# A LayerNorm, linear-attention and MLP block on one core: a new order for every engine, the block map on GpSimd, another queue for one tile, a fourth u tile

## The chip, the cores and the metric

The kernel runs on one core of a Trainium2 chip. The core has five engines with their own instruction queues: TensorE (PE; PEld is its weight load), VectorE (DVE), ScalarE (ACT), GpSimd (POOL) and SyncE (SP, which only issues transfers here). Each runs its queue strictly in order and waits at an instruction until its inputs are there. Transfers are issued from SP's and from ScalarE's queue. The metric is the time of one execution on the device in microseconds; the median of three runs of the kernel before is 239.16 (239.09 to 239.38).

## What is computed

Sequence 2048, width 640, 32 heads of 20, hidden width 1728, all inputs in bfloat16:

```python
qkv = (x @ wqkv) ...                      # q, k, v of 32 heads, 20 wide
pq = einsum("bhsd,hdf->bhsf", q, w_phi)   # pk the same of k
phi_q = concat([softmax(pq), softmax(-pq)])   # phi_k the same of pk
kv = einsum("bhsf,bhsd->bhfd", phi_k, v)
num = einsum("bhqf,bhfd->bhqd", phi_q, kv)
den = einsum("bhqf,bhf->bhq", phi_q, phi_k summed over s) + 1e-6
h  = x + (num / den) @ wo                 # of layernorm(x)
out = h + silu(layernorm(h) @ w1) @ w2
```

## The kernel before

The 2048 rows are 16 tiles of 128 rows (tile number t). All weights stay in SBUF. Nothing is scheduled by a planner at build time: `ORDER` (lines 25 to 64) is a string of words, each word calls one function `op_<name>`, and every engine receives its instructions in the order in which the words stand. `vp.1@6` is `op_vp(1)` with PSUM bank 6 (two-bank results take 6 and 7); there are eight banks. A word's last letter picks the engine or queue: `.a` ScalarE, `.v` DVE, `.p` GpSimd, `.s` SP's queue.

Four stages follow each other and overlap a little.

*Head.* Loads: `lx.a.b` tiles a to b-1 of x, `lk` chunks of the K weights (five of 128 rows), `lv` the V weights, `lp` the small weights w_phi. On GpSimd `mk` makes mask5 and `mo` writes the ones columns of ten V tiles. On DVE `ph` (L195) spreads w_phi into `phb`, the block map: 128 x 5 x 8 x 20 elements, the product of w_phi and mask5. TensorE runs dummy matmuls (`wm`, L262), then transposes the K weights (`wt`, five 128x128, L316), `wc` copies them from PSUM, `fk` (L331) multiplies them with phb and `fc` copies the result to Wfk, the K weights with w_phi folded in. For each x tile `st` takes statistics (two L267 and one L268, DVE), `rs` makes 1/std (L275, a pow on GpSimd), `xn` normalizes (L291 on DVE or L296 on ScalarE). The first four tiles are transposed on TensorE (`xt`, L302, copied by `xc`), the other twelve by a transposing DMA on SP's queue (`xd`).

*Projections.* `kp` and `vp` (both L364) multiply a tile with Wfk and with wv; `ke` takes exp of plus and minus pk (ScalarE), `kr` sums and inverts (DVE), `kn` (L407) normalizes: `.p` all 1280 elements on GpSimd, `.q` 960 there and 320 on DVE (L411), `.b` half each. `vc` copies v. `cc` (L420) adds the tile's phi_k, v product into bank 7. `gk` and `gc` make Wfq as `fk` and `fc` made Wfk, from Q weights that `lq` loads transposed; `qp` (L451, `.0` and `.1` two banks, `.2` one) gives pq of four tiles and `qe` (L461) its exp, EqT. `kc` and `km` spread kv into KVBD; `mc` and `mt` make the mask for that on GpSimd and DVE. `close` frees the memory of the stage.

*Attention.* `dp` (L486) multiplies EqT with KVBD into four banks. `dw` (DVE; L500, L501, L507, L510) makes from it `u`, an f32 tile of 128 x 672, and then the four banks are free; u lies in a pool of three buffers. `dr` inverts the denominators (L515), two `do` (L521, DVE or GpSimd) give `o`, and only then is a u buffer free. `td` transposes o by DMA, `op` (L548) multiplies with wo, `oa` (L557, DVE) adds x, `sq` (ScalarE) and `sr` (GpSimd, L570 to L580) make the second LayerNorm's numbers, `hn` normalizes on DVE (L587) or on ScalarE (L595, with one more GpSimd instruction, L592), `hd` transposes by DMA.

*MLP.* `up` (L627, L637) over groups of 2, 4, 4, 4 and 2 tiles, `ua` silu (L649), `yp` (L673) and `yh` (L686) the down projection, `yo` and `yz` the last add and the store.

A pool's buffers and the eight transfer lanes make further waits: a transfer takes one of eight completion lanes in turn, and waits for the transfer before it in the same lane.

Of the kernel before, what the change touches and what calls it, by code (L numbers as in the profile page):

```python
# [64 lines left out]
"""

@with_exitstack
def kernel(
# [40 lines left out]
    first = early.enter_context(tc.tile_pool(name="first", bufs=1, side="right"))  # L109
# [51 lines left out]
    tl = {}  # L161
# [10 lines left out]
    def wk2():  # L172
        return late["work"]
# [17 lines left out]
            base=DH, pattern=[[6 * DH - 128, C], [DH, 8]], channel_multiplier=-1,  # L191
        )

    def op_ph():
        nc.vector.tensor_tensor(  # L195
            phb[:],
            phr[:].unsqueeze(2).to_broadcast([P, C, 8, DH]),
            mask5[:].unsqueeze(3).to_broadcast([P, C, 8, DH]),
            op=ALU.mult,
        )  # L200
# [277 lines left out]
    def op_dp(t):  # L478
        g, i = t // GT, t % GT
        b = at.pop(0)  # L480
        ps = mm[:, b : b + 4, :]
        for s in range(2):
            for r in range(C):
                for k in range(4):
                    lo = 32 * k
                    nc.tensor.matmul(  # L486
                        ps[:, k, (8 * s + H0[r]) * 22 : (8 * s + H0[r] + NJ[r]) * 22],
                        EqT[g][lo : lo + 32, s, r, i * P : (i + 1) * P],
                        KVBD[lo : lo + 32, s, r, 0 : NJ[r], :].rearrange("p j c -> p (j c)"),
                        start=(s == 0 and r == 0),  # L490
                        stop=(s == 1 and r == C - 1),
                        skip_group_check=True,
                    )
        tl["dp", t] = [ps[:, :, 176 * s : 176 * (s + 1)].rearrange("p k (h c) -> p k h c", c=22) for s in range(2)]

    def op_dw(t, how="p"):
        A = tl["dp", t]
        first = A[0][:, :, :, 0:21]
        w = sm.tile([P, 4, 8], F32, name="w")
        nc.vector.reciprocal(w[:], A[1][:, :, :, 21])  # L500
        nc.vector.tensor_tensor(w[:], w[:], A[0][:, :, :, 21], op=ALU.mult)  # L501
        if how == "c":
            kept = wk2().tile([P, 4, 8, 21], F32, name="kept", bufs=1)
            nc.scalar.copy(kept[:], first)
            first = kept[:]
        u = wk2().tile([P, 4, 8, 21], F32, name="u", bufs=3)
        nc.vector.tensor_tensor(  # L507
            u[:], A[1][:, :, :, 0:21], w[:].unsqueeze(3).to_broadcast([P, 4, 8, 21]), op=ALU.mult,
        )
        nc.vector.tensor_tensor(u[:], u[:], first, op=ALU.add)  # L510
# [229 lines left out]
```

## Time and profile before

| what | value |
|---|---|
| median of 3 runs | 239.16 us (239.09 to 239.38) |
| the profiled execution | 238.86 us |
| its span, first to last instruction | 237.2 us |
| TensorE busy | 229.9 us |
| DVE, ScalarE, GpSimd busy | 133.7, 114.9, 92.9 us |
| first projection matmul | 10.65 us |
| first dp | 69.27 us |
| mean of a dw's four DVE instructions | 0.35, 0.19, 0.86, 0.85 us |
| mean of kn with 1280, 960, 640 elements on GpSimd | 2.40, 1.81, 1.86 us |
| do on GpSimd, on DVE | 0.75, 0.49 us |

Times in a row are from the span's start. A line of a timeline gives start, duration, engine, source line, operation, `out<-in`, count, and in brackets the engine's idle time before it and what ended it. In the chain of waits each row is a start, a duration and what ran. In the slices each digit is the busy share of a fortieth of the span in tenths. TensorE's matmuls overlap, and their ends are modelled, so the distance between starts is the better measure of their pace.

### The profile page before, as it was taken

The page shows a single profiled execution, that of the slowest core. Times are in us where ns is not written, and L with a number is a line of the kernel's source. Part 1 is how long each engine was busy: PE and PEld are TensorE (multiplying, and loading weights), DVE is VectorE, ACT ScalarE, POOL GpSimd, SP SyncE. Part 2 cuts the span into 40 slices and gives each one's busy share as a digit, 9 for nine tenths or more (in the row PEclk, how much of TensorE's full clock was granted, in tenths as well). Part 3 has the DMA queues.
Part 4 walks back from the last instruction along what each step waited for, and adds up shares of the span by engine and source line. Part 5 has one row for each costly group of instructions (what it writes and reads, how often), then busy time and mean ns, then how long its engine had stood idle before and what let it go on. Part 6 is the DMA issues. An engine that isn't in the chain of part 4 may idle for free.

```text
span 237.2 us, 6320 instructions
## 1 busy us (share of the span) xinstructions
PE 229.9 (97%) x2672; PEld 147.6 (62%) x2672; DVE 133.7 (56%) x257; ACT 114.9 (48%) x172; POOL 92.9 (39%) x184
## 2 busy tenths in 40 slices
PE   6899999999999999999999999999999999999995
PEld 2677777777544555886754645556654657688762
DVE  3899999899838989988878504321203000220032
ACT  3788998866866575664054254654014240013000
POOL 7656897798923454188071600534000100000000
PEclk9999999999999999999999999999999999999999
DMA  7964768495001849123734411103211100020012
GB/s 209 305 239 92 128 118 184 120 249 175 3 6 31 179 80 197 37 53 62 113 83 86 83 30 28 29 12 75 72 41 55 28 28 3 28 83 3 0 60 83
DMA packets 44845, 20.68 MB, mean 87 GB/s; under 512 B 34448, under 2 KB 44304, under 8 KB 44816
## 3 DMA queue, kind: packets, MB, share of 16 engines
q1 hardware_dynamic: 43728, 19.88, 36.1%
q10 hardware_dynamic: 1088, 0.39, 0.7%
q8 instruction: 21, 0.34, 0.6%
q14 instruction: 8, 0.07, 0.1%
HBM read 9.61 MB, written 2.62 MB: 52 GB/s over the span
## 4 chain that ended last, share of the span: by engine, by line
PE 88%; DVE 4%; POOL 4%; ACT 1%; DMA 1%; issue 1%; DVEq 0%; POOLq 0%
PE mm L673 24%; PE mm L627 23%; PE mm L364 18%; PE mm L548 8%; PE mm L451 7%; PE mm L486 3%; PE mm L420 2%; ACT EqT L461 1%; DMA X<-in_A_x_dram 1%; PE mm L686 1%; DVE u L507 1%; DVE u L510 1%; PE mm L637 1%; POOL RS L275 1%; PE mm L331 1%
## 5 line engine op out<-in xcount | busy, mean ns | idle before, releaser
L627 PE MATMUL mm<-HnT,w 128*128 128x512 bf16 (+1 forms) x325 | 59.1, 337 | 0.0
L649 ACT ACTIVATE shT<-mm 128x1024 bf16<-128x1024 f32 (+2 forms) x29 | 27.7, 963 | 64.3 <-PE mm L627 48.8
L673 PE MATMUL mm<-w,shT 128*128 128x320 bf16 (+2 forms) x416 | 58.5, 299 | 0.0
L673 PEld LDWEIGHTS <-shT 128*128 128x128 bf16 x416 | 39.7, 98 | 17.7 <-issue 0.8
L627 PEld LDWEIGHTS <-w 128*128 128x128 bf16 x325 | 31.3, 98 | 22.8 <-issue 0.3
L694 DVE TENSOR_TENSOR ob<-mm,X 128x640 bf16<-128x640 f32 x15 | 12.0, 817 | 47.0 <-PE mm L673 29.3
L364 PEld LDWEIGHTS <-XnT 128*128 128x128 bf16 x320 | 30.7, 98 | 11.8 <-issue 0.2
L407 POOL TENSOR_TENSOR Ek<-Ek,Sk 128x1280 bf16<-128x1280 bf16 (+2 forms) x16 | 34.6, 2184 | 3.1 <-DVE Sk L400 2.2
L557 DVE SCALAR_TENSOR_TENSOR X<-mm,X 128x640 bf16<-128x640 f32 x16 | 13.1, 823 | 21.5 <-PE mm L548 21.3
L397 DVE TENSOR_REDUCE Sk<-Ek 128x64 f32<-128x1280 bf16 x16 | 23.3, 1456 | 1.6 <-ACT Ek L389 1.6
L548 PE MATMUL mm<-wo,ot 128*128 128x320 bf16 x160 | 23.9, 299 | 0.2 <-ACT EqT L461 0.2
L521 POOL TENSOR_TENSOR o<-u,rd 128x320 bf16<-128x320 f32 x20 | 14.7, 752 | 22.7 <-DVE rd L515 14.4
L364 PE MATMUL mm<-Wfk,XnT 128*128 128x320 bf16 x160 | 23.4, 299 | 0.0
L451 PE MATMUL mm<-XnT,Wfq 128*128 128x512 bf16 x100 | 23.3, 380 | 0.0
L461 ACT ACTIVATE EqT<-mm 128x1024 bf16<-128x1024 f32 (+1 forms) x24 | 19.6, 884 | 7.4 <-PE mm L451 7.4
L364 PE MATMUL mm<-wv,XnT 128*128 128x320 bf16 x160 | 23.2, 299 | 0.0
L389 ACT ACTIVATE Ek<-mm 128x640 bf16<-128x640 f32 x32 | 20.6, 710 | 3.2 <-PE mm L364 2.7
L548 PEld LDWEIGHTS <-ot 128*128 128x128 bf16 x160 | 15.4, 98 | 7.4 <-issue 0.7
L565 ACT ACTIVATE sq<-X 128x640 bf16<-128x640 bf16 x16 | 11.7, 730 | 9.3 <-DVE X L557 7.7
L267 DVE BATCH_NORM_STATS2 stats<-X 128x6 f32<-128x320 bf16 x32 | 13.7, 468 | 3.8 <-DMA X<-in_A_x_dram 3.8
L577 POOL TENSOR_SCALAR hm<-hst,hm 128x1 f32<-128x1 f32 x16 | 4.6, 290 | 28.0 <-ACT sq L565 27.0
L451 PEld LDWEIGHTS <-Wfq 128*128 128x128 bf16 x100 | 9.1, 98 | 9.9
(78 smaller groups left out, 214.0 us busy)
## 6 DMA issues: line engine op xcount, KB each, us to landing
out_dram<-ob SPq DMA_DIRECT2D x15, 160.0 KB, 1.8
w<-in_B_w_dram SPq DMA_DIRECT2D x6, 360.0 KB, 5.2
X<-in_A_x_dram SPq DMA_DIRECT2D x3, 640.0 KB, 6.6
w<-in_B_w_dram SPq DMA_DIRECT2D x5, 320.0 KB, 4.9
wk<-in_A_wqkv_dram SPq DMA_DIRECT2D x4, 160.0 KB, 4.2
wv<-in_A_wqkv_dram SPq DMA_DIRECT2D x1, 480.0 KB, 7.3
wo<-in_A_wo_dram SPq DMA_DIRECT2D x1, 480.0 KB
w<-in_B_w_dram SPq DMA_DIRECT2D x1, 480.0 KB, 4.0
```

Of the source, the lines that this page charges most:

```text
L267: nc.vector.bn_stats(stats[:, k, :], X[:, t, k * 320 : (k + 1) * 320])
L364: nc.tensor.matmul(ps[:, half, 0:320], tok(XnT[t // GT], t)[:, c, :], W[:, c, half * 320 : (half + 1) * 320], start=(c == 0), stop=(c == C ...
L389: nc.scalar.activation(Ek[:, s, :].rearrange("p (a n) -> p a n", a=2), tl["kp", t][:, :, 0:320], AF.Exp, scale=1.0 - 2.0 * s,)
L397: nc.vector.tensor_reduce(Sk[:], tl["ek", t][:].rearrange("p s (h f) -> p (s h) f", f=DH), axis=AX.X, op=ALU.add,)
L407: nc.gpsimd.tensor_tensor(Ek3[:, 0:n], Ek3[:, 0:n], Sk[:, 0:n].unsqueeze(2).to_broadcast([P, n, DH]), op=ALU.mult,)
L451: nc.tensor.matmul(ps[:, k, :], Wfq[:, c, r * P : (r + 1) * P], XnT[g][:, c, :], start=(c == 0), stop=(c == C - 1),)
L461: nc.scalar.activation(E[:, s, rs[0] : rs[-1] + 1, :], tl["qp", g, i][:, 0 : len(rs), :], AF.Exp, scale=1.0 - 2.0 * s,)
L521: (nc.vector if eng == "v" else nc.gpsimd).tensor_tensor(tl["o", t][:, a * 320 : (a + 1) * 320].rearrange("p (h f) -> p h f", f=DH), tl["u ...
L548: nc.tensor.matmul(ps[:, half, 0:320], tl["ot", t][:, c, :], wo[:, c, half * 320 : (half + 1) * 320], start=(c == 0), stop=(c == C - 1),)
L627: nc.tensor.matmul(ps[:, i * W : (i + 1) * W], w1[:, c, fc * P : (fc + 1) * P], HnT[g][:, c, 0:W], start=(c == 0), stop=(c == C - 1), skip ...
L649: nc.scalar.activation(sh[:, a:b], tl["up", g, k][:, 0 : b - a], AF.Silu)
L673: nc.tensor.matmul(ps, shT[g][:, fc * W + i * P : fc * W + (i + 1) * P], w2[:, fc, a:b], start=first and fc == 0, stop=last and fc == FC - ...
```

## The change

`ph` takes an engine as argument, and the new order calls `ph.p`: the product for phb is now GpSimd's. Tile 1 of x (`lx.1.2`) is issued from ScalarE's queue, third there, where the last chunk of the K weights (`lk.4.5`) stood; that chunk now goes last on SP's queue, behind tiles 2 and 3 of x (`lx.2.4`). `mc`, the second mask, stands among the kn on GpSimd rather than in the head. The u pool has four buffers. The variant `how="c"` of `dw` copies the whole PSUM result; every `dw` word in both orders ends in `.p`. `mo` stands before `mk`. The whole order is new: among others 13 kn are `.p` (10 before), one is `.q` (4 before); 11 hn run on ScalarE (7 before), 10 xn (9 before); on TensorE xt.0 comes before wt.2, wt.3, wt.4 and all fk (before: after four of the five fk); the head has three dummies of 256 columns more. Loads of x come as tiles 4 to 7, 12 to 15, 8 to 11 (before: 8 to 11, 4 to 7, 12 to 15).

```diff
-lx.0.1.a lk.0.1.s lp.a lx.1.2.s lk.4.5.a lk.1.2.s lk.2.3.s lk.3.4.s mk mo wm.512@7 wm.512@7 wm.512@7
-wm.512@7 wm.512@7 wm.512@7 wm.512@7 wm.512@7 wm.512@7 wm.256@7 wt.0@0 st.0 rs.0.1 wm.256@2 wm.128@2 wt.4@1
-ph ta mc st.1 wc.0.a wt.1@2 lx.2.4.s wc.1.v fk.0@4 wt.2@3 wc.2.v lx.8.12.s wc.4.a fc.0.a fk.4@6 fc.4.a
-rs.1.2 xn.0.v fk.1@0 fc.1.a wt.3@2 wc.3.v fk.2@4 fc.2.a xt.0@3 xn.1.v xc.0.v st.2 rs.2.3 st.9 fk.3@6 fc.3.a
-xn.2.v xt.1@2 st.8 xc.1.a rs.8.10 kp.0@0 ke.0 kp.1@4 lv.0.3.s ke.1 lv.3.5.s xt.2@3 xc.2.a vp.1@6 lq.1.s st.3
+mo mk lx.0.1.a lp.a lx.1.2.a lk.0.1.s lk.1.2.s st.0 rs.0.1 st.1 ta wm.512@7 wm.512@7 wm.512@7 wm.512@7
+wm.512@7 wm.512@7 wm.512@7 wm.512@7 wm.512@7 wm.256@7 wt.0@0 wc.0.a ph.p xn.0.v lx.2.4.s rs.1.2 wt.1@1
+wc.1.a wm.256@3 xt.0@2 xc.0.a lk.2.3.s wm.256@4 wm.256@4 wm.128@4 wt.2@3 st.2 rs.2.3 wc.2.a xn.1.v wm.256@6
+fk.0@4 lk.3.4.s wt.3@6 wc.3.v fk.1@0 lk.4.5.s lx.4.8.s fc.0.a fc.1.a wt.4@7 wc.4.v lv.3.5.s fk.2@2 fc.2.a
+fk.3@4 fk.4@6 xn.2.v fc.3.v st.3 fc.4.a xt.1@0 rs.3.4 xc.1.a xt.2@1 xc.2.a kp.0@2 ke.0 st.5 kp.1@4 kp.2@6
...
-qe.0.0 qp.0.2@6 cc.7 close kc qe.0.2 qp.3.0@2 l2.4.6.s l2.6.8.s km.1 km.0 dp.0@4 dw.0.p dr.0 do.0.0.p l1.2.s
-l1.3.s qe.3.0 do.0.1.p qp.1.0@0 dp.1@2 qe.1.0 dw.1.p dr.1 do.1.1.p qp.1.1@6 dp.3@0 dw.3.p qe.1.1 do.1.0.v
-dr.3 do.3.0.p do.3.1.p qp.2.0@4 qe.2.0 dp.2@0 dw.2.p dr.2 qp.1.2@6 qe.1.2 td.0 do.2.0.p l1.4.s l1.5.s op.0@4
+gk.4@2 cc.6 ke.10 cc.0 cc.12 kn.8.p cc.5 gc.4.a l1.4.s kp.13@4 ke.13 l2.8.10.s kp.14@0 ke.14 kr.14 qp.0.0@2
+vp.9@4 qe.0.0 l1.2.s vp.10@0 vc.10.a qp.0.1@2 vc.9.a vp.14@0 kn.9.b vc.14.a cc.11 qe.0.1 kn.15.p cc.15
+kn.14.p cc.8 kr.10 kn.10.p cc.10 qp.0.2@6 qe.0.2 kr.13 kn.13.b mt cc.14 cc.9 cc.13 kc km.0 km.1 qp.3.0@4
+qe.3.0 lo.0.2.s close dp.0@0 dw.0.p dr.0 do.0.1.p qp.1.1@6 qe.1.1 dp.1@0 dw.1.p dr.1 qp.2.0@4 do.0.0.p
+do.1.1.v qe.2.0 dp.3@0 dw.3.p qp.1.0@6 dr.3 do.3.1.v qp.2.2@4 l2.2.4.s dp.2@0 qe.1.0 dw.2.p dr.2 qp.1.2@5
+lh.s qe.2.2 td.0 do.1.0.p td.1 op.0@6 oa.0 do.3.0.p td.3 qe.1.2 dp.4@0 dw.4.p l2.4.6.s sq.0 do.2.0.p op.1@4
+qp.2.1@6 oa.1 dr.4 do.4.1.v dp.6@0 sr.0 dw.6.p dr.6 hn.0.a do.2.1.p td.2 do.4.0.p qe.2.1 sq.1 sr.1 hn.1.v
+qp.3.1@4 qe.3.1 op.3@6 qp.3.2@0 qe.3.2 td.4 oa.3 sq.3 do.6.1.v do.6.0.p dp.5@2 dw.5.p op.2@6 oa.2 op.4@0
+oa.4 dp.9@2 sr.3 hd.0 dw.9.p hd.1 dr.5 up.0.2@6 ua.0.2 l1.1.s hn.3.a dr.9 up.0.3@0 ua.0.3 l2.6.8.s td.6
+do.5.0.v dp.7@2 dw.7.p up.0.0@6 ua.0.0 op.6@0 dr.7 dp.13@2 do.5.1.p td.5 oa.6 do.9.1.p do.9.0.p dw.13.p
...
-    def op_ph():
-        nc.vector.tensor_tensor(
+    def op_ph(eng="v"):
+        (nc.vector if eng == "v" else nc.gpsimd).tensor_tensor(
...
-        first = A[0][:, :, :, 0:21]
+        if how == "c":
+            kept = wk2().tile([P, 4, 352], F32, name="kept", bufs=1)
+            nc.scalar.copy(kept[:], tl["ps", t])
+            A = [kept[:, :, 176 * s : 176 * (s + 1)].rearrange("p k (h c) -> p k h c", c=22) for s in range(2)]
...
-        u = wk2().tile([P, 4, 8, 21], F32, name="u", bufs=3)
+        u = wk2().tile([P, 4, 8, 21], F32, name="u", bufs=4)
...
-        nc.vector.tensor_tensor(u[:], u[:], first, op=ALU.add)
+        nc.vector.tensor_tensor(u[:], u[:], A[0][:, :, :, 0:21], op=ALU.add)
```

More of the change, by code (lines that the diff above doesn't have):

```diff
@@ new lines @@
+lx.8.12.s xd.5 st.13 vp.2@4 xn.7.a vc.2.a kp.3@0 xd.4 xd.7 vp.1@2 xn.6.v lq.2.s lq.0.s rs.12.14 st.8 st.11
+st.10 rs.10.12 st.9 rs.8.10 kr.1 vp.3@4 kn.1.p ke.3 xd.6 ke.2 vp.5@0 vc.5.a xn.11.a xn.13.v vp.4@6 vc.3.a
+vc.4.a kp.5@0 ke.5 kr.3 kn.3.p vc.1.a xn.8.a kp.7@4 ke.7 kp.4@6 ke.4 gk.0@0 vp.7@2 vc.7.a st.15 xd.11 xn.9.a
+vp.11@4 st.14 rs.14.16 xn.15.a kr.2 kn.2.p kr.4 kn.4.p vc.11.v kr.7 kr.0 kn.7.p gc.0.a l1.0.s vp.6@6 mc
+xn.12.a xn.10.v kp.11@2 ke.11 kn.0.p kp.6@4 l1.3.s vc.6.a kr.5 xn.14.a xd.13 vp.13@0 lq.1.s xd.8 kp.8@2
@@ new lines @@
+l2.10.13.s vc.13.a cc.3 l1.5.s ke.6 kr.6 cc.4 kn.6.p kr.11 cc.1 cc.2 cc.7 kn.5.p ke.8 xd.9 kp.9@0 ke.9 xd.12
+kp.12@4 ke.12 kr.12 kn.12.p gk.2@2 gc.2.a xd.15 kp.15@0 ke.15 vp.15@4 kr.8 vp.12@2 vc.15.a gk.1@0 gc.1.a
+vp.8@4 vc.8.a lo.2.5.s xd.10 kp.10@0 vc.12.a l2.0.2.s lq.3.s gk.3@4 gc.3.a xd.14 kn.11.q lq.4.s kr.9 kr.15
+gk.4@2 cc.6 ke.10 cc.0 cc.12 kn.8.p cc.5 gc.4.a l1.4.s kp.13@4 ke.13 l2.8.10.s kp.14@0 ke.14 kr.14 qp.0.0@2
+vp.9@4 qe.0.0 l1.2.s vp.10@0 vc.10.a qp.0.1@2 vc.9.a vp.14@0 kn.9.b vc.14.a cc.11 qe.0.1 kn.15.p cc.15
@@ new lines @@
+yp.0.1 yo.0 yp.1.0 yo.1 td.7 dp.14@4 dw.14.p up.1.1@0 ua.1.1 do.8.1.p dr.14 up.1.6@2 ua.1.6 do.8.0.p sq.6
+sr.6 do.14.0.v dp.10@4 dw.10.p up.1.0@0 ua.1.0 up.1.5@2 sq.9 hn.6.v hd.6 do.14.1.p ua.1.5 up.1.2@4 do.12.0.v
+ua.1.2 op.7@6 oa.7 dp.11@0 td.8 up.1.4@4 dw.11.p dr.10 do.10.1.v up.1.3@6 ua.1.3 do.12.1.p td.14 do.13.1.v
+dr.11 td.12 op.14@0 oa.14 sq.7 ua.1.4 op.8@2 oa.8 sq.8 op.12@6 yp.3.0@0 yp.5.0@4 sr.8 do.10.0.p td.10 td.13
+oa.12 yh.1.0@2,6 yh.1.1 hn.8.a hd.8 yp.5.1 yo.5 yp.2.1 sr.9 hn.9.v sr.7 hn.7.a hd.9 hd.7 yp.3.1 yo.3 op.10@4
@@ new lines @@
+yp.2.0 yo.2 yp.4.1 oa.10 up.2.6@0 ua.2.6 dp.15@2 dw.15.p yp.4.0 yo.4 op.13@0 dr.15 do.15.0.v do.11.0.p
+up.2.0@2 up.2.4@4 ua.2.4 up.2.1@6 ua.2.1 oa.13 up.2.2@0 do.11.1.v ua.2.2 sq.14 do.15.1.p sr.14 sq.13 sr.13
+td.15 sq.12 sr.12 up.2.5@4 ua.2.5 up.2.3@6 td.11 op.11@0 ua.2.0 ua.2.3 yp.9.0@4 yp.6.0@2 op.15@6 yp.6.1
+oa.11 sq.10 sr.10 hn.13.a hd.13 sq.11 hn.12.a hd.12 hn.14.v hd.14 oa.15 sq.15 sr.11 hn.11.a hd.11 yh.2.0@0
+yo.6 hn.10.v hd.10 sr.15 yh.2.1@6 hn.15.a hd.15 yp.7.1 yp.7.0 yp.8.0 yp.9.1 yo.9 up.3.4@2 yp.8.1 yo.7
@@ L65 @@
+up.4.0@4 ua.4.0 up.4.2@6 up.3.1@4 ua.3.4 ua.3.1 up.3.0@2 up.4.3@4 yo.8 ua.3.0 ua.4.3 up.3.3@0 up.3.2@2
+ua.3.2 ua.4.2 up.4.1@4 ua.4.1 up.3.6@2 ua.3.6 yh.4.0@6,4 yp.14.0 up.3.5@2 yp.15.1 yp.15.0 yp.14.1 yo.14
+ua.3.3 ua.3.5 yp.11.1@0 yp.10.1@2 yp.10.0 yp.12.0@6 yh.3.0 yo.15 yo.10 yh.3.1@4,5 yp.11.0 yo.11 yp.12.1
+yo.12 yp.13.0 yz.13.0.s yp.13.1 yz.13.1.a
 """
@@ L501, in op_dw @@
         nc.vector.tensor_tensor(w[:], w[:], A[0][:, :, :, 21], op=ALU.mult)
[L502 to L505, printed above, removed]
-        u = wk2().tile([P, 4, 8, 21], F32, name="u", bufs=3)
+        u = wk2().tile([P, 4, 8, 21], F32, name="u", bufs=4)
         nc.vector.tensor_tensor(
```

35 lines of the change are left out of this document (4 added, 31 removed).

## The prediction

> **What bounds the kernel now.** I read the page first (shares, slices, chain), then what TensorE waited for, then the timeline of the first 11 us, then the chain through the attention stage.
>
> ```profile
> span 237.2 us, 6320 instructions
> ...
> PE 229.9 (97%) x2672; PEld 147.6 (62%) x2672; DVE 133.7 (56%) x257; ACT 114.9 (48%) x172; POOL 92.9 (39%) x184
> ...
> DVE  3899999899838989988878504321203000220032
> ...
> PEclk9999999999999999999999999999999999999999
> ```
>
> TensorE is busy 97% of the span at full granted clock, and DVE is near 90% until slice 20 (about 120 us). The matmuls that compute something are the same in both kernels, so the time can change only by when dense matmul work begins and by how often TensorE then waits. What it waited for:
>
> ```profile
> PE mm L316 <- DMA wk<-in_A_wqkv_dram: 1.4, 1, 1.4
> PE mm L486 <- DVE u L510: 1.4, 4, 0.5
> PE mm L302 <- DVE xn L291: 0.6, 1, 0.6
> PE mm L548 <- ACT EqT L461: 0.2, 1, 0.2
> ```
>
> Columns: total, times, longest. Two waits lie in the head (1.4 for a weight chunk, 0.6 for xn), five in the attention stage. None lies between 11 and 69 us: the projections run without a gap.
>
> ```profile
> 1.25 0.41 SPq L233 DMA_DIRECT2D X<-in_A_x_dram  x1
> 1.72 0.55 ACTq L233 DMA_DIRECT2D wk<-in_A_wqkv_dram  x1
> 5.02 0.99 DVE L195 TENSOR_TENSOR phb<-phr,mask 128x800 bf16<-128x800 bf16 x1
> 6.24 0.73 PE L316 MATMUL mm<-ident,wk 128*128 128x128 bf16 x10 [1.45 <-DMA wk<-in_A_wqkv_dram]
> 10.25 0.45 PE L302 MATMUL mm<-ident,xn 128*128 128x128 bf16 x5 [0.61 <-DVE xn L291]
> 10.65 2.89 PE L364 MATMUL mm<-Wfk,XnT 128*128 128x320 bf16 x20
> ```
>
> The head ends at 10.65, when kp.0 (L364) starts. Line 4 is wt.4: TensorE stood until 6.24 for the chunk that ScalarE's queue sent third, at 1.72. The first and the last wait of the attention stage, in the chain:
>
> ```profile
> 71.51 0.86 DVE u L510
> 72.38 0.04 issue
> 72.42 0.51 PE mm L486 x34
> ...
> 122.63 0.69 POOL o L521
> 123.33 0.02 issue
> 123.35 0.87 DVE u L507
> 124.22 0.02 issue
> 124.24 0.86 DVE u L510
> 125.11 0.04 issue
> 125.15 0.46 PE mm L486 x35
> ```
>
> dp.1 (72.42) needs the banks that dw.0 frees. dp.10 (125.15) waits for dw.15, whose u tile had to be freed by GpSimd's do.12.1 (L521, 122.63): three u tiles were not enough there.
>
> **The change, part by part.**
>
> *Head.* Tile 1 of x moves from SP's second place to the third place of ScalarE's queue. In the completion events of the trace it landed at 4.3 in the old place; the transfer of the same size in the new place landed at 6.2. Bounds 4.3 and 6.2; I take 6.2, as it is the same queue, place and issue time. In the new order DVE does st.1 before xn.0, so xn.0 now waits for tile 1: 6.2 + 1.15 (two L267, one L268: 3.77 to 4.92) + 0.45 (L291) + 0.05 = xt.0 at 7.9, against 8.72 before. Behind xt.0 TensorE's queue holds, before kp.0: wt.2, wt.3, wt.4, xt.1, xt.2 and xt.0 itself (6 x 0.28, chain), five fk (0.32 each, chain, L331 x6) and four dummies (256 columns about 0.11, one of 128: 0.38 in all). Sum 3.66, so 11.55, and 0.1 because the last fk needs wc.4 (0.49 on DVE) right behind wt.4: kp.0 at 11.65. Before, kp.0 started at 10.65 with xt.2 still to do (0.28). The head costs 11.65 - 0.28 - 10.65 = **+0.7** (with the 4.3 bound: xn.0 is then set by GpSimd's pow, xt.0 near 6.9, kp.0 near 10.7, so -0.2; an upper end of +1.2 if the landing slips by 0.5).
>
> What is hidden there: the block map phb on GpSimd. Nearest rows: L407 (1280 elements, bf16, 4.67 for two, 1.8 ns an element) gives 1.45; L521 (320 elements, 0.75) gives 1.9. I take 1.45, the row with the same output type. It starts behind rs.0.1, between 6.1 (pow from 5.17, 0.55 as its other single-column rows, L277 0.26) and 6.8 (pow 1.24, as it was beside DVE's phb), and ends by 8.7 at the latest; fk.0 wants it at 8.8 (xt.0 7.9 plus 0.9 of transposes and dummies). What covers it is the late xt.0; with an early tile 1 it would cost up to 0.5. The last wk chunk now waits for a DMA lane and is issued at about 3.76. Before, the X transfer issued at 3.76, with the same bytes up to its end, landed at 9.1; wt.4 wants the chunk at 9.75. Moving mo ahead of mk costs nothing: GpSimd does both before 4.5, and the pow comes at 5.17.
>
> [...]
>
> *Projections, 11 to 69 us.* DVE loses phb (0.99) and three L411 parts (0.45 each). GpSimd gains three kn of 1280 instead of 960 elements (2.31 - 1.81 = 0.5 each), phb, and the second mask (2.5 us, 6.71 to 9.20 before) in the middle of its kn chain. In 12.2 to 66.9 GpSimd was busy 44.4 of 54.7 us, so the room is there on average. The end decides: kp.14 ends near 56.1, ke.14 and kr.14 (1.3 + 1.95) let kn.14 start at 59.4; kn.14, kn.10, kn.13 (2.3, 2.3, 1.9, with 0.6 for kr.10) end at 66.5; cc.13 stands at 67.4. Slack 0.9; before, the last kn ended 0.2 ahead of cc.7. DVE had 4.4 us of idle there and gets more. ScalarE (45.3 of 54.7) gains one xn (0.82). SP's twelve xd and five lq keep their number; the first due, xd.5, is issued near 17 and lands in 2.6 for vp.5 near 22.8. Cost 0.
>
> *Attention stage, 69 to 126 us.* The waits view shows 1.6 us; measured by late starts of the matmuls (the array also drains at each wait) it is 2.3: dp.1 0.45, dp.3 0.27, dp.2 0.37, two for EqT 0.24 and 0.33, the last dp 0.64. In the new order, with dw 2.36 and 3.0 us from a dp to its banks' release: dp.1 (one double qp of 2.16 as cover) keeps 0.45, dp.3 0.35 (0.27 before); do.1.1 is queued on DVE before dw.3, so dw.3 ends 0.25 later, which dp.2 has room for. dp.2 has 3.24 of qp ahead: 0. Both EqT waits go, since op.0 and its followers take banks whose qe is done earlier. up.0.2 gets 0.4: it needs oa.2, which stands on DVE behind dw.5 (2.36). dp.7 0.15, small ones 0.2. The 0.64 goes with the fourth u tile. New sum 1.55, change **-0.75**; bounds -1.5 (only dp.1 and dp.3 left) and 0. Four more hn on ScalarE (0.92 each) lie in a stage where it was busy 31 of 57 us; each adds an L592 (0.26) on GpSimd, 26 of 57.
>
> *The rest.* The `kept` path is not reached: every dw word ends in p. After 126 us the old kernel has no wait and the new order keeps 25 groups of row-tiled matmuls, as before, so those switches cost the same; 0. The tail (last add, last DMA) is unchanged.
>
> **Sum.** +0.7 - 0.75 = about 0 on 238.86 (span 237.2 and 1.66 around it). The median of the runs is 0.3 above that execution, so the forecast for the median is 239.2: no change. A measurement of this kernel can tell about 0.2% (0.48 us) from none.
>
> **Rivals.**
> 1. *Tile 1 lands early* (faster). The old place landed at 4.3, and a queue's turn is not fixed. Head -0.2 to 0, attention -0.75: 238.3; down to 237.7 if the attention waits fall to dp.1 and dp.3. Against it: the third transfer of that queue was late at the same issue time. [...]
> 2. *GpSimd's chain ends last before dp.0* (slower). One mechanism: phb, the mask and 13 full kn make GpSimd late at cc.10 and cc.13. It decides once a full kn averages over 2.45 us (0.9 slack over the six of the last stretch); the mean of L407 in this form is 2.40, the longest 2.60. At 2.60 over the 13, with 2.31 assumed, it is 3.8 less 0.9 late, of which DVE's order hides about half: +1.5, so 240.7. For it: DVE works beside it all the time; against: pairs ran at 2.3.
> 3. *The clock falls in the head* (slower). TensorE now idles from about 4.7 to 7.9, 3.2 us; before, 1.45 us did no harm. At the start the dummies were 0.43 apart until 3.34 and 0.22 after, so 2.5 us at half pace cost 1.25: +1.3, 240.5. [...]
> 4. *The u tile does not help*: its wait returns as another DVE wait. Only the head's +0.7 stays: 239.9.
>
> **How the numbers follow.** Forecast (238.7 to 239.7) 0.40, of it 0.03 faster, 0.30 same, 0.07 slower. Rival 1: 0.27, faster. Rival 2: 0.20, rival 3: 0.08, rival 4: 0.05, all slower. Faster 0.30, same 0.30, slower 0.40. The range runs from rival 1's middle to rival 2's price: 238.0 to 240.7. Forecast's own range: 238.7 to 239.7.
>
> **What would show it.** kp.0 starting near 11.65 with xt.0 near 7.9 behind st.1 (head right); xt.0 before 7.2 (rival 1). The phb multiply at 1.4 to 1.9 us on GpSimd, ended before fk.0. No TensorE wait from 12 to 70 us; one on `Ek` from GpSimd at the last cc would be rival 2. Dummies and transposes at 0.1 us pitch after 7.9: rival 3. In the waits view u at dp.1 and dp.3 only, and none on do. It is wrong if a wait outside these places passes 0.5 us.

## The result and the profile after

The changed kernel takes 242.19 us (median of five runs, 241.06 to 242.63), the kernel before 239.16 (five runs beside it, 239.09 to 239.62). The ratio is 1.0115, 95% interval 1.0086 to 1.0143: 3.0 us slower, where 239.2 us and a range of 238.0 to 240.7 had been forecast. One execution of the third experiment below (243.06 us) counts as slow, and its median and ratio leave it out.

The profiled execution took 242.63 us, 3.77 more than that of the kernel before. First the page of the changed kernel: span, busy times, the slices of DVE and the granted clock.

```profile
span 240.5 us, 6303 instructions
...
PE 230.3 (96%) x2655; PEld 150.0 (62%) x2675; DVE 132.6 (55%) x248; ACT 118.9 (49%) x177; POOL 95.7 (40%) x189
...
DVE  2699999995867998977785741353013120000232
...
PEclk9799999999999999999999999999999999999999
```

TensorE has the same work, and DVE less. What is new is the 7 in the second slice of the clock (6 to 12 us): it was 9 in every slice before. The waits of TensorE in the changed kernel (total, times, longest):

```profile
PE mm L303 <- DVE RS L273: 2.1, 1, 2.1
PE mm L332 <- issue: 1.6, 1, 1.6
...
PE mm L487 <- DVE u L511: 0.7, 2, 0.5
PE mm L628 <- DMA HnT<-hn: 0.6, 1, 0.6
PE mm L452 <- issue: 0.6, 4, 0.2
```

The chunk wait of 1.4 us in the head is gone, and one of 2.1 us ahead of xt.0 stands in its place. The second row is a kind that the kernel before did not have: 1.6 us, once, released by nothing that the profile shows. The last row, by contrast, is no wait: ahead of each of its four matmuls stand two weight loads and one matmul record, so a matmul was not recorded, and the row is absent in kernels 12 and 13 below, whose profiles have one matmul for each load. The timeline of TensorE in the changed kernel, head and then the place of that gap:

```profile
5.77 0.27 PE L263 MATMUL mm<-const-bfloat16-1.0 128*128 128x256 bf16 x1
8.10 0.45 PE L303 MATMUL mm<-ident,xn 128*128 128x128 bf16 x5 [2.06 <-DVE RS L273]
...
9.68 0.74 PE L317 MATMUL mm<-ident,wk 128*128 128x128 bf16 x5
...
13.38 0.84 PE L365 MATMUL mm<-Wfk,XnT 128*128 128x320 bf16 x5
...
45.45 0.32 PE L332 MATMUL mm<-phb,wk 128*128 128x140 bf16 x3
47.40 0.32 PE L332 MATMUL mm<-phb,wk 128*128 128x80 bf16 x3 [1.63 <-issue]
```

xt.0 starts at 8.10 and kp.0 at 13.38. The five transposes of a weight chunk that take 0.45 at full clock (the row at 8.10 is of the same shape) take 0.74 at 9.68: they start 0.107 us apart instead of 0.056. The same head in windows of the changed kernel (busy time of PE, PEld, DVE, ACT, POOL, then the granted clock, the DMA share and GB/s):

```profile
8.00:9.20 1.20, 1.10 (x16) 1.05 (x17) 1.13 (x6) 0.61 (x2) 0.81 (x2) 0.93 0.91 318
9.20:13.30 4.10, 4.10 (x50) 4.10 (x49) 2.35 (x6) 3.04 (x6) 0.94 (x2) 0.60 1.04 399
13.40:17.00 3.60, 3.60 (x30) 2.61 (x28) 3.46 (x12) 3.57 (x7) 0.86 (x3) 1.00 0.20 80
```

By the spacing of the transposes the clock is at half from about 9.0 to 12.4 us, in the densest part of the head. Both marks, the clock and the gap, lie in stages where the prediction had costs of +0.7 and 0.

Where the 3.77 us of the profiled pair come from: kp.0 is 2.73 later (13.38 against 10.65); from there to dp.0 the changed kernel takes 1.30 more (dp.0's first matmul at 73.23 against 69.20), which is 1.80 at the gap, by starts of matmuls, less 0.50; from dp.0 to the end it takes 0.70 less (167.26 against 167.96); and the time outside the span is 2.14 instead of 1.70 (spans of 240.49 and 237.16 in the traces), which is 0.44.

### The profile page after: what moved, and what is told of

It is laid out like the page before. It is cut to its first block, busy times and chain, and to the rows that moved or that the text cites. A ratio compares the mean times of both kernels' runs of the same rounds, so it can differ in the third digit from the quotient of the medians.

```text
span 240.5 us, 6303 instructions
## 1 busy us (share of the span) xinstructions
PE 230.3 (96%) x2655; PEld 150.0 (62%) x2675; DVE 132.6 (55%) x248; ACT 118.9 (49%) x177; POOL 95.7 (40%) x189
## 4 chain that ended last, share of the span: by engine, by line
PE 85%; DMA 4%; DVE 4%; issue 2%; ACT 2%; POOL 0%; ACTq 0%; DVEq 0%; POOLq 0%
PE mm L628 24%; PE mm L674 23%; PE mm L365 18%; PE mm L549 6%; PE mm L452 4%; PE mm L487 2%; DMA X<-in_A_x_dram 2%; PE mm L421 2%; DMA HnT<-hn 2%; PE mm L332 2%; ACT EqT L462 1%; PE mm L638 1%; PE mm L687 1%; DVE u L508 1%; DVE u L511 1%
## 5 line engine op out<-in xcount | busy, mean ns | idle before, releaser
L628 PE MATMUL mm<-HnT,w 128*128 128x512 bf16 (+1 forms) x315 | 57.8, 335 | 1.2 <-DMA HnT<-hn 0.6
L408 POOL TENSOR_TENSOR Ek<-Ek,Sk 128x1280 bf16<-128x1280 bf16 (+2 forms) x16 | 35.7, 2260 | 2.6 <-DVE Sk L401 2.3
L522 POOL TENSOR_TENSOR o<-u,rd 128x320 bf16<-128x320 f32 x20 | 16.0, 808 | 37.3 <-DVE rd L516 30.6
L452 PE MATMUL mm<-XnT,Wfq 128*128 128x512 bf16 x91 | 22.3, 379 | 0.9 <-issue 0.6
L596 ACT ACTIVATE hn<-X,hm 128x640 bf16<-128x640 bf16 x11 | 10.1, 916 | 9.6 <-POOL hm L593 9.5
L508 DVE TENSOR_TENSOR u<-mm,w 128x672 f32<-128x672 f32 x16 | 13.7, 858 | 1.4 <-DVE w L506 0.3
```

Source lines behind the costliest of these rows:

```text
L408: nc.gpsimd.tensor_tensor(Ek3[:, 0:n], Ek3[:, 0:n], Sk[:, 0:n].unsqueeze(2).to_broadcast([P, n, DH]), op=ALU.mult,)
L452: nc.tensor.matmul(ps[:, k, :], Wfq[:, c, r * P : (r + 1) * P], XnT[g][:, c, :], start=(c == 0), stop=(c == C - 1),)
L508: nc.vector.tensor_tensor(u[:], A[1][:, :, :, 0:21], w[:].unsqueeze(3).to_broadcast([P, 4, 8, 21]), op=ALU.mult,)
L522: (nc.vector if eng == "v" else nc.gpsimd).tensor_tensor(tl["o", t][:, a * 320 : (a + 1) * 320].rearrange("p (h f) -> p h f", f=DH), tl["u ...
L628: nc.tensor.matmul(ps[:, i * W : (i + 1) * W], w1[:, c, fc * P : (fc + 1) * P], HnT[g][:, c, 0:W], start=(c == 0), stop=(c == C - 1), skip ...
```

## The experiments

Three theories at the start. A: TensorE's idle stretch ahead of xt.0 makes the clock fall. B: loads that the change issues earlier hold up the transfer by which TensorE gets its instructions, so that it runs dry at 45 us. C: the late tile 1 is the cause of the head. The rival of them all is that the new order itself, with its sequence of matmuls and copies, is slower. Each kernel was timed against the kernel before on the same chip. The mean granted clock of a run tells whether the clock fell: 3.41 us at half of it (0.50 from 9.03 to 12.44 us in the changed kernel) are 1.7 of 237 us, a mean of 0.993.

| | kernel | median (us) | ratio to before, interval | runs below 0.998 in clock |
|---|---|---|---|---|
| | changed kernel | 242.19 | 1.0115 (1.0086 to 1.0143) | 4 of 5 |
| 1 | dummies before xt.0 | 240.76 | 1.0083 (1.0051 to 1.0116) | 1 of 6 |
| 2 | four loads later | 240.68 | 1.0059 (1.0034 to 1.0084) | 7 of 9 |
| 3 | tile 1 on SP's queue | 240.77 | 1.0068 (1.0043 to 1.0093) | 7 of 12 |
| 4 | 2 and 3 | 240.28 | 1.0031 (1.0013 to 1.0050) | 7 of 12 |
| 5 | 1 and 2 | 239.51 | 1.0006 (0.9997 to 1.0016) | 0 of 11 |
| 6 | 4, phb on DVE | 238.06 | 0.9946 (0.9934 to 0.9958) | 0 of 5 |
| 7 | 5, three u tiles | 239.89 | 1.0021 (1.0011 to 1.0030) | 0 of 11 |
| 8 | before, two loads earlier | 240.57 | 1.0060 (1.0043 to 1.0077) | 0 of 6 |
| 9 | 6, loads early again | 238.84 | 0.9979 (0.9962 to 0.9995) | 0 of 12 |
| 10 | before, four u tiles | 239.12 | 0.9994 (0.9985 to 1.0002) | 0 of 11 |
| 11 | before, fewer dummies | 239.52 | 1.0015 (0.9999 to 1.0032) | 1 of 12 |
| 12 | changed, phb on DVE | 241.16 | 1.0075 (1.0050 to 1.0100) | 4 of 6 |
| 13 | 1, lo.2.5 later | 239.55 | 1.0013 (1.0004 to 1.0022) | 0 of 12 |
| 14 | 1, the other three loads later | 240.18 | 1.0041 (1.0027 to 1.0056) | 0 of 6 |

**1. Dummies in the idle stretch.**

```diff
-wc.1.a wm.256@3 xt.0@2
+wc.1.a wm.512@3 wm.512@3 wm.512@3 wm.512@3 wm.512@3 wm.512@3 wm.512@3 wm.512@3 xt.0@2
```

> The changed kernel with eight 512-column dummies where one of 256 columns stood between wt.1 and xt.0, so that TensorE has work from 5.8 to about 7.5 us. Clock theory: the granted clock stays at 1.00 behind xt.0, the transposes of wt.3 and wt.4 come 0.056 us apart instead of 0.107, kp.0 starts near 11.7 instead of 13.38, and the time falls by 1.6 to 1.8, to a median near 240.5. Rival, head late by tile 1 and its own order only: kp.0 stays near 13.4 or comes later by what the dummies add, the median stays at 242.2 or above.

240.76 us, 1.43 less than the changed kernel (1.6 to 1.8 were expected), and the clock fell in one run of six instead of four of five. TensorE in this kernel's head, and the clock in four windows around its gap:

```profile
5.79 1.91 PE L263 MATMUL mm<-const-bfloat16-1.0 128*128 128x512 bf16 x8
8.43 0.45 PE L303 MATMUL mm<-ident,xn 128*128 128x128 bf16 x5 [0.73 <-DVE RS L273]
```

```profile
40.00:44.00 4.00, 3.90 (x177) 3.02 (x177) 3.97 (x4) 3.37 (x6) 3.79 (x7) 1.00 1.40 202
44.00:46.00 2.00, 0.02 (x1) 0.02 (x1) 1.93 (x4) 0.42 (x1) 1.97 (x2) 1.00 0.42 110
46.00:48.00 2.00, 2.00 (x14) 1.48 (x14) 0.54 (x1) 1.28 (x3) 2.00 (x2) 0.65 1.17 289
48.00:50.00 2.00, 2.00 (x10) 1.10 (x8) 1.84 (x2) 0.67 (x4) 1.45 (x1) 0.50 0.93 91
```

The dummies end before tile 1 is ready and leave 0.73 us idle ahead of xt.0, and kp.0 starts at 12.21 instead of 13.38. The one run in which the clock did fall is the profiled one (243.34 us), and there it fell behind the gap at 44 to 46 us, which is 2.08 us long in it: one more case of theory A, at another place, seen in this one profile.

**2. The loads later.** lo.2.5 (480 KB of wo) and l1.5 go behind lq.4; l2.10.13 and l2.0.2 behind td.1.

```diff
-l2.10.13.s vc.13.a cc.3 l1.5.s ke.6
+vc.13.a cc.3 ke.6
-vp.8@4 vc.8.a lo.2.5.s xd.10 kp.10@0 vc.12.a l2.0.2.s lq.3.s gk.3@4 gc.3.a xd.14 kn.11.q lq.4.s kr.9
+vp.8@4 vc.8.a xd.10 kp.10@0 vc.12.a lq.3.s gk.3@4 gc.3.a xd.14 kn.11.q lq.4.s lo.2.5.s l1.5.s kr.9
-td.1 op.0@6
+td.1 l2.10.13.s l2.0.2.s op.0@6
```

> The changed kernel with four weight loads moved later on SP's queue: lo.2.5 and l1.5 behind lq.4, l2.10.13 and l2.0.2 behind td.1. Fetch theory (TensorE ran out of instructions at 45.6 us, because the 16 KB packet that brings the next ones was held up by the transfers of 36 to 45 us): that packet starts before 43, the gap of 1.63 us in gk is gone or below 0.3, and the time falls by 1.3 to 1.8, to a median near 240.6. Rival, a data wait that the trace does not name (the Q weights, a bank, phb): the gap stays within 0.3 of 1.63 and the median at 242.2.

240.68 us; the gap is gone from the waits, and the head is as it was (2.44 us idle ahead of xt.0). Seven runs at a mean clock of 0.984 to 0.993 took 240.42 to 242.29 us, the two at 1.000 took 239.12 and 239.52: a fall costs about 1.4 us here.

**3 and 4. Tile 1 on SP's queue**, second there, and lk.4.5 third on ScalarE's, as before the change; kernel 4 has the later loads as well.

```diff
-lx.0.1.a lp.a lx.1.2.a lk.0.1.s lk.1.2.s
+lx.0.1.a lp.a lk.4.5.a lk.0.1.s lx.1.2.s lk.1.2.s
-fk.1@0 lk.4.5.s lx.4.8.s
+fk.1@0 lx.4.8.s
```

> The changed kernel with tile 1 of x back on SP's second place and the last chunk of the K weights back on ScalarE's third, as before the change. Clock theory: tile 1 lands near 4.3, xn.0 is then set by GpSimd's pow (done at 5.9), xt.0 starts near 7.0, TensorE idles under 2 us ahead of it and the clock stays at 1.00; kp.0 near 10.8; the time falls by 2.3 to 2.6, to a median near 239.7, with the gap in gk left. Rival, the drop has nothing to do with the idle stretch: the clock still falls, kp.0 near 12.4, median near 241.3.

> Both of the edits before this one: tile 1 on SP's second place and the four loads later. If head and fetch are the two losses and nothing else is, they add: kp.0 near 10.8, no gap in gk, the time 4.0 us below the changed kernel's, a median near 238.2, that is 1.0 below the kernel before, which is the gain of the attention stage. Rival, the attention stage's gain was lent by the delays ahead of it: median at 239.0 or above.

Both miss: 240.77 and 240.28 us. Tile 1 lands early (4.65 us in kernel 4), but xt.0 starts at 8.06 all the same, behind 2.20 us of idle. xn.0 in the changed kernel, then DVE and GpSimd in kernel 4:

```profile
7.65 0.39 DVE L292 TENSOR_SCALAR xn<-X,MV,RS 128x640 bf16<-128x640 bf16 x1
```

```profile
6.31 1.70 DVE L291 TENSOR_SCALAR xn<-X,MV,RS 128x640 bf16<-128x640 bf16 x1
```

```profile
6.30 1.52 POOL L195 TENSOR_TENSOR phb<-phr,mask 128x800 bf16<-128x800 bf16 x1
```

xn.0, which takes 0.39 us in the changed kernel, takes 1.70 here: it starts with phb on GpSimd and ends right behind it (8.01 against 7.82). Theory C falls as it stood; tile 1's gain is eaten by phb. In kernel 4, with no gap, five runs at a clock of 1.000 took 238.74 to 239.28 (median 238.95), seven at 0.993 took 240.25 to 240.70 (median 240.45): the fall of the clock alone is 1.5 us.

**5. Both repairs, 1 and 2.**

> The changed kernel with both repairs: eight dummy products of 512 columns before xt.0 (as in the first experiment) and the four weight loads later (as in the second). If the loss consists of the half clock in the head and the late instruction packet alone: no gap on TensorE at 45 us, dp.0 at about 70.3 us (12.2 us for kp.0 as with the dummies, and the 58.06 us from there to dp.0 that the kernel with later loads shows), nearly every run with a mean clock of 0.999 or 1.000, and 238.7 us (238.3 to 239.3). If there is a third loss behind them, that neither repair touches: 239.8 or more with the clock at 1.000. If the clock falls whatever TensorE does, for the chip's own reasons: about half of the runs again at 0.993 and 240.3 or more.

239.51 us, every run of eleven at a clock of at least 0.998. The two repairs remove 2.7 of the 3.0 us, and the clock does not fall by itself. The median is 0.2 above the range expected: TensorE still waits 0.2 us at 44 us, and the time outside the span is 2.1 us here too, 0.4 more than in the kernel before. The spans alone are 236.9 to 237.8, as those of the kernel before (237.1 to 237.7).

**6. phb on DVE behind xn.0, on top of 4.**

```diff
-wt.0@0 wc.0.a ph.p xn.0.v lx.2.4.s
+wt.0@0 wc.0.a xn.0.v ph lx.2.4.s
```

> The kernel with tile 1 on SyncE's queue and the loads later, and the block map phb made by VectorE right behind xn.0 instead of by GpSimd. In the last run xn.0 took 1.70 us where it lay beside phb on GpSimd (6.3 to 7.9 us), against 0.39 us where phb was over. If the two engines hinder each other: xn.0 takes 0.39 to 0.45 us again, xt.0 starts at 6.8 us instead of 8.06, TensorE idles no more than 1.5 us in the first 8 us, the clock stays at 1.000 in most runs, and the time is 238.2 us (237.8 to 238.7), below the kernel before the change. If xn.0 was slow for another reason (its own data, the first use of a buffer): xn.0 stays at 1.7 us, xt.0 at 8, and the time is 240.3 with the clock at 0.993 in half of the runs.

238.06 us, faster than both kernels; all five runs at 1.000. DVE and TensorE in its head:

```profile
6.08 0.39 DVE L291 TENSOR_SCALAR xn<-X,MV,RS 128x640 bf16<-128x640 bf16 x1
6.39 0.98 DVE L195 TENSOR_TENSOR phb<-phr,mask 128x800 bf16<-128x800 bf16 x1
```

```profile
6.04 0.45 PE L316 MATMUL mm<-ident,wk 128*128 128x128 bf16 x5 [0.86 <-DMA wk<-in_A_wqkv_dram]
...
6.53 0.45 PE L302 MATMUL mm<-ident,xn 128*128 128x128 bf16 x5
...
10.77 0.43 PE L364 MATMUL mm<-Wfk,XnT 128*128 128x320 bf16 x2
```

xn.0 is back at 0.39, so the two engines did hinder each other; xt.0 comes at 6.53, kp.0 at 10.77, almost as early as before the change (10.65). What makes this kernel faster than the old one lies behind dp.0: 167.0 us to the end against 168.0.

**7. Three u tiles in kernel 5**, `bufs=4` back to `bufs=3`.

> The kernel with both repairs (dummies, loads later), with three u tiles instead of four. If the fourth u tile is what made the attention stage shorter by 0.7 us: 0.5 us (0.3 to 0.8) more than the same kernel with four, and waits of PE on u of 1.2 us or more in sum. If the gain comes from the new order alone: the same time within 0.2 us.

239.89 us, 0.38 more than kernel 5. One wait that no kernel with four tiles has returns in its list, on the way to the last dp, at 127.5 us:

```profile
PE mm L627 <- DVE u L510: 0.4, 1, 0.4
```

The two waits on u behind dp.0 (0.7 in sum) are there with three tiles and with four. From dp.0 to the end this kernel takes 167.46 us, kernel 5 166.98 and the kernel before 167.96. So by these profiles the fourth tile is worth 0.48 of the 0.98 us that are gained behind dp.0, and the new order the other 0.50. The whole times differ by less, since the time outside the span is 1.7 us here and 2.1 in kernel 5.

**8. The gap made in the kernel before**, by two loads issued some 7 us earlier and nothing else.

```diff
-gk.2@6 st.15 xd.5
+gk.2@6 st.15 xd.5 l2.0.2.s l2.2.4.s
-kn.4.q l2.0.2.s l2.2.4.s gc.4.a
+kn.4.q gc.4.a
```

> The kernel before the change with one edit: the two loads l2.0.2 and l2.2.4 are issued some 7 us earlier, behind xd.5, so that they land while TensorE's third instruction packet (at 40.97 us in the kernel before) is under way. If TensorE ran dry in the changed kernel because loads held up that packet: the packet starts at 42 to 44 us, TensorE stands still 1.0 to 2.0 us with no releaser ahead of the 961st of its recorded instructions (43.5 us in the kernel before), and the time is 240.5 us (240 to 241.2). If the gap belonged to the new order of TensorE and not to the loads: no such gap and 239.1 us.

240.57 us, 1.33 more. In the profiled pair the stretch from kp.0 to dp.0, which has the gap, is 0.92 longer; kp.0 itself comes 0.44 later, which this edit does not touch (see 10). TensorE's weight loads in this kernel:

```profile
43.41 0.37 PEld L364 LDWEIGHTS <-XnT 128*128 128x128 bf16 x3
44.90 1.20 PEld L364 LDWEIGHTS <-XnT 128*128 128x128 bf16 x10 [1.12 <-issue]
```

The old order runs dry at the same place; its matmuls stand idle for 0.79 us there. (The row of the matmuls names ScalarE's exp as releaser there; the last of these ended at 44.58, 0.3 us ahead of the restart.)

**9. Kernel 6 with the loads where the change puts them.**

> The best kernel so far (tile 1 on SyncE's queue, phb on VectorE; 238.06 us) with the four weight loads back where the change puts them. Its head leaves no idle stretch that takes the clock, so this run has the price of the late instruction packet by itself. If the loads hold the packet up: it starts after 43 us instead of 39.91, TensorE stands still ahead of its 961st recorded instruction for 1.2 to 2.1 us, and the time is 239.8 us (239.3 to 240.3). If the gap needed the changed head as well: no gap and 238.1 us.

238.84 us, 0.78 more than kernel 6 and less than expected: the runs spread from 237.61 to 239.63, and the profiled one (238.13) has a gap of only 0.18 us. The spread suggests that the loads cost something different from run to run here; only one run has a trace.

**10. Four u tiles in the kernel before**, `bufs=3` to `bufs=4`.

> The kernel before the change with four u tiles and nothing else. If the fourth tile is worth what it was in the changed order (0.4 us in the pair with both repairs): 238.8 us (238.5 to 239.1), and the wait on u at 125 us (0.5 us) shrinks. If it is worth something only in the new order: 239.2 us.

239.12 us, no difference (at most 0.36 faster by the interval). In its profile the wait at 125 us is gone, u stands in the waits with 0.8 instead of 1.4 us, and from dp.0 to the end it takes 0.32 us less. But kp.0 starts at 11.02 instead of 10.65, with the same instructions in the head (in kernel 8, with the same head again, at 11.09), so that one profile's head can hide such a gain. Whether that is why the median does not follow is not settled.

**11. The kernel before with fewer dummies.**

```diff
-wm.512@7 wm.512@7 wm.512@7 wm.512@7 wm.512@7 wm.512@7 wm.256@7 wt.0@0 st.0 rs.0.1 wm.256@2 wm.128@2 wt.4@1
+wm.512@7 wm.512@7 wm.512@7 wm.512@7 wm.256@7 wt.0@0 st.0 rs.0.1 wt.4@1
```

> The kernel before the change without the last two of its eight dummy products of 512 columns and without the two small ones behind wt.0. None of them computes anything, and the next transposes wait for the transfer lk.4.5, which lands at 6.2 us either way; only TensorE's idle stretch ahead of them grows from 1.45 to about 2.1 us. If an idle stretch of that length within 3.4 us takes the clock: most runs at a mean clock of 0.993, transposes at 0.107 us apart somewhere between 6.5 and 14 us, and 240.6 us (240.2 to 241.0) in those runs. If the clock falls in the changed kernel for another reason: 239.2 us and 1.000.

Missed in the frequency: 239.52 us, and one run of twelve at 0.993 (240.00), which is the profiled one. Its windows:

```profile
3.90:7.30 3.40, 1.25 (x22) 1.05 (x21) 3.15 (x8) 0.97 (x2) 2.52 (x8) 1.00 0.96 320
7.30:10.70 3.40, 3.40 (x38) 3.40 (x36) 2.27 (x6) 2.48 (x5) 2.53 (x7) 0.50 0.90 327
10.80:14.00 3.20, 3.20 (x32) 2.30 (x31) 2.94 (x10) 2.57 (x5) 0.81 (x2) 1.00 1.10 197
```

The clock rose at 3.9 us, TensorE was busy 1.25 of the next 3.4 us, and then it was at half for the 3.4 us that follow. So in the old order too the clock fell behind an idle stretch (2.15 of these 3.4 us were idle). That it seldom does may be a matter of where the stretch lies behind the rise of the clock: here the clock had risen before TensorE stopped at 4.4 us, and in the profiles it rises anywhere from 3.5 to 6.0. That is argued from this one run, not shown.

**12. The changed kernel with phb on DVE**, the edit of 6 alone.

> The changed kernel with phb on VectorE behind xn.0 and nothing else. In the changed kernel xn.0 comes when phb is over on GpSimd (7.65 us against 7.78), since tile 1 lands at 6.58. If GpSimd's phb therefore costs nothing there: xt.0 again at 8.1 us, TensorE idle 2.0 us ahead of it, the clock at 0.993 in most runs and the gap at 45 us as before, 242.2 us (241.6 to 242.7). If GpSimd's phb is the cause of the late head by itself: xt.0 before 7.5 us and 240.5 us or less.

xt.0 starts at 8.33 behind 2.18 us of idle, and the clock fell in four of six runs: phb on GpSimd is not what makes the head late. But the time is 241.16 us, 1.0 under the changed kernel and under the range expected: its profile has no gap at 45 us (TensorE's third packet starts 1.84 us behind instruction 705, see below), and the time outside the span is 0.3 us less. Why this edit does either is not settled; on the gap, the issue times below give a hint.

**13 and 14. Which load**, in the kernel with the dummies: lo.2.5 later alone, and then only the other three.

```diff
-vp.8@4 vc.8.a lo.2.5.s xd.10
+vp.8@4 vc.8.a xd.10
-xd.14 kn.11.q lq.4.s kr.9
+xd.14 kn.11.q lq.4.s lo.2.5.s kr.9
```

> The kernel of the first experiment (changed kernel with eight dummies of 512 columns, so that its clock holds; 240.76 us, TensorE still for 2.08 us ahead of its 961st recorded instruction), with the one load lo.2.5 (480 KB) behind lq.4 and the other three loads where the change puts them. In that kernel lo.2.5 was issued at 39.47 us, 0.95 us ahead of the 705th instruction, and the third packet started 3.2 us behind that instruction; where the loads come later it starts 0.9 to 1.0 us behind it. If lo.2.5 is the load that holds the packet up: packet 1 to 1.5 us behind the 705th instruction, no gap over 0.4 us, 239.5 us (239.1 to 239.9). If the earlier two loads of w (l2.10.13, l1.5) do it: the gap stays over 1 us and the time is 240.6 us.

> The counterpart: lo.2.5 where the change puts it, and l2.10.13, l1.5 and l2.0.2 later. If lo.2.5 alone holds the packet up: packet 3 us behind the 705th instruction, a gap of 1.2 to 2.1 us, 240.7 us (240.2 to 241.1). If the other loads do it: no gap and 239.5 us. If it takes both, as a sum of traffic: gaps of 0.5 to 1 us in both of these runs and 240.0 us in both.

239.55 and 240.18 us, beside 240.76 with all four loads early. Without lo.2.5 there is no gap, whatever the other three do; with it alone there is one of 0.81 us:

```profile
44.54 0.70 PE L364 MATMUL mm<-Wfk,XnT 128*128 128x320 bf16 x4 [0.81 <-issue]
```

So in this order lo.2.5 makes the gap. That the loads ahead of it lengthen it (2.08 with them in kernel 1) rests on one profile of each kernel, and kernel 14 just missed what was expected of it (1.2 to 2.1 us, 240.2 or more).

**What ties the runs on the gap together.** The instructions of TensorE come in 21 transfers of 16,384 bytes ("q8 instruction: 21, 0.34" in the list of queues: number and MB), and the trace has 5,330 matmuls and weight loads: some 254 for each. Counting these and the few semaphore instructions between them from 0, TensorE stops ahead of number 961 in every kernel that has the gap, the two with seven more dummies (1 and 14) and the old order (8) included, so that it is another matmul of the program each time. Times from the trace in us, the idle time as the matmuls show it:

| kernel | number 705 runs | third packet starts | number 961 starts | idle ahead of it |
|---|---|---|---|---|
| before | 39.49 | 40.97 | 43.53 | 0 |
| changed | 41.64 | 45.00 | 47.40 | 1.63 |
| 1 | 40.42 | 43.60 | 45.98 | 2.08 |
| 2 | 42.21 | 43.07 | 46.17 | 0 |
| 3 | 42.67 | 45.85 | 48.16 | 1.24 |
| 8 | 39.92 | 42.16 | 44.90 | 0.79 |
| 9 | 39.20 | 41.18 | 43.61 | 0.18 |
| 12 | 41.86 | 43.70 | 46.08 | 0 |
| 13 | 39.94 | 40.83 | 43.45 | 0.02 |
| 14 | 40.25 | 42.12 | 44.54 | 0.81 |

Without loads in the way, the packet starts 0.9 to 1.1 us after number 705 in the new order (2, 4 to 7, 13), which is 256 ahead of 961 and so about one packet, and 1.5 to 1.7 after it in the old one; with them 1.8 to 3.4. In the changed kernel it took 0.93 us from 45.00 and TensorE went on 1.47 after its end; 1, 3, 9 and 14 show 1.39 to 1.48, and kernel 8 1.20. SP's transfers of the changed kernel show what went ahead of it:

```profile
41.17 0.58 SPq L234 DMA_DIRECT2D wo<-in_A_wo_dram  x1
41.99 1.21 SPq L310 DMA_TRANSPOSE XnT<-xn  x1
```

lo.2.5 was issued at 41.17, 0.5 us ahead of number 705, and landed at 47.62, 6.4 us later. The issue time goes with the delay in all six profiles that have this load early: issued 0.47, 0.83 and 0.95 us ahead of number 705 (changed, 3, 1), the packet starts 3.2 to 3.4 behind it; issued 1.44 to 1.50 ahead (14, 12, 9), 1.8 to 2.0. That may be why the gap is small in 9 and 14 and absent in 12; no run sets the issue time by itself. Nor does any show by what means a load holds the packet up.

## Why the prediction failed, step by step

**Head, tile 1.** Predicted to land at 6.2, landed at 6.58; xt.0 predicted at 7.9, came at 8.10. Right but for 0.2 in this profile. In the kernels with the same place (1, 2, 5, 12, 13, 14) the tile landed between 6.25 and 7.15, so 6.2 was the early end and not the late bound; kernel 5, with the clock at full, has kp.0 at 12.04 instead of 11.65.

**Head, from xt.0 to kp.0.** Here it failed. The sum of 3.66 + 0.1 us is right at full clock: with the dummies it is 3.78 (8.43 to 12.21). In the changed kernel it is 5.28, since the clock was at half for 3.4 us. This is rival 3, given 0.08, and it came true in four runs of five. Its price was too low as well: 1.25 forecast, 1.4 and 1.5 between runs of one kernel with and without the fall. The false step was to hold the fall for unlikely, where the kernel before shows only that 1.45 us did no harm: what length takes the clock was not shown by any run then. Nor was the stretch the one expected, 3.2 us from 4.7. It was 2.06 us (6.05 to 8.10), because the dummies ran at half pace (0.427 us apart) and the clock rose only at 5.62; and it was enough. In the heads of the sixteen profiles of this case the clock falls 3.4 us behind its rise where these 3.4 us hold 1.8 us or more of idle (changed: 2.06, from 5.62 to 9.03; 2, 3, 4, 11, 12), and stays where they hold 1.6 or less (before: 1.45; kernel 9: 1.57, its rise read from the spacing of the dummies). Once down, it rose after another 3.4 us, in kernel 3 only after twice that. The other changes lie on the same step of 3.4 us: rise at 3.9, fall at 7.3, rise at 10.7 in kernel 11; in kernel 1 the fall at 46.62 comes twelve times 3.41 behind the rise at 5.66.

**phb on GpSimd.** Predicted 1.45, taken 1.52, from 6.26 to 7.78, 1.5 times DVE's 0.99; fk.0 came at 9.08. It was hidden as said, and by what was said, the late tile 1. The price "up to 0.5" for an early tile 1 was on the wrong step: what phb delays is not fk.0 but xn.0, which takes 1.70 beside it instead of 0.39 (kernel 4). There xn.0 starts 0.01 behind phb and ends 0.2 behind it; by what means the one holds up the other no run shows. The rival of an early tile 1 (238.3) left this out: with the loads later as well, kernel 4 took 238.95 where its clock held, and 238.06 came only with phb back on DVE (kernel 6).

**Projections, "Cost 0".** The second failure. The step counted engines and listed SP's twelve xd and five lq, and left out the other loads that the new order puts among them. lo.2.5, issued between two xd, held up TensorE's third instruction packet (3.36 us behind number 705, against 0.89 in kernel 13); 1.80 us in the profiled run. By medians the later loads are worth 1.25 (kernel 1 to 5) to 1.5 us (changed to 2). GpSimd's chain, rival 2, was no matter: a full kn averages 2.38 us, under the 2.45 from which it was to decide, and TensorE waits for no Ek at the last cc. The rest of the stage is 0.50 shorter, of which 0.28 was forecast (xt.2).

**Attention stage, -0.75.** Right in the sum: -0.70 in the profiled run, -1.0 in the repaired kernels (2, 4, 5 and 6: 167.0 us from dp.0 to the end). By parts: waits on u 0.48 and 0.23 where 0.45 and 0.35 were expected; none at the last dp; up.0.2 0.6 instead of 0.4 (0.3 to 0.5 in the repaired kernels and in 1 and 12 to 14). The split was partly luck: the fourth u tile was said to be worth 0.64 and is worth 0.48 (kernel 7 against 5), and the new order without it was to gain 0.11 and gains 0.50 there.

**Outside the span.** Forecast at 1.66 us, measured at 2.14. It is 2.0 to 2.2 in the changed kernel and in 1 to 5, 13 and 14, and 1.65 to 1.9 in the others. Nothing in the trace shows why; it stays open.

**The sum** in the profiled pair: head 2.73 instead of 1.00 (kp.0 at 11.65), projections +1.30 instead of -0.28, attention stage -0.7 as forecast, outside +0.44 instead of 0.

## What to carry to other kernels

An idle stretch of TensorE cost about its length here (1.80 us by starts of matmuls at the gap of 1.63), and 1.4 to 1.5 us of slow clock on top where 1.8 us or more of the 3.4 us behind the rise of the clock were idle: where something must be waited for in a head, try dummies that end before it comes; they ended 0.73 us ahead of xt.0 and saved 1.4 us (kernel 1 against the changed one). A load that moves can get in the way of TensorE's own instruction transfers, as lo.2.5 did (a gap of 0.81 us with it alone, 0.02 without it, kernels 14 and 13): behind a dense burst of short matmuls (260 to 307 recorded instructions in 1.3 us here), keep SP's big loads out of the microseconds in which the next packet is fetched. And before an elementwise operation goes from DVE to GpSimd, look at what DVE does in the same microseconds (xn.0: 1.70 instead of 0.39 us), not only at who waits for the result.

## What the runs showed of the hardware that had not been expected

TensorE starved for instructions, by all that ties these runs together: for up to 2.08 us (kernel 1), in these profiles always ahead of recorded instruction 961. The packets that bring them have 16,384 bytes, some 254 records each. The third one's delay was hidden where it started up to 1.84 us behind number 705 (save 0.2 us or less in 5, 7 and 13), and not from 1.87 on (0.18 us in kernel 9 to 2.08 in 1).

A gap of 2.08 us in the middle of the program took the clock as an idle head does (kernel 1: 0.50 from 48 to 50 us), so that this stall was paid for twice. The changed kernel's gap of 1.63 us did not (granted clock 1.00 from 45.5 to 47.5 us). Counted in steps of 3.41 us from the rise at 5.62, it lies across two of them, with some 0.8 us in each; that this spared the clock is the author's estimate.

The half pace at the very start, when the dummies are 0.427 us apart until 3.4 to 6 us, shows as a granted clock of 1.00 in the windows (2 to 6 us of the changed kernel); only the spacing of matmuls tells it. The best kernel of the study is number 6, the new order with tile 1 on SP's queue, phb on DVE and the four loads later: 238.06 us against 239.24 beside it.
